# Decode attention with an FFN: W_down loaded by 1 KB rows, and one V tile loaded in five pieces instead of one

## The chip, the cores and the metric

The kernel runs on one core of one Trainium2 chip. The metric is the device time of one execution in microseconds (us), lower is better, taken as the median of several executions. On one core no other die is there to compare with, so a kernel's runs are called fast when they agree with each other; all timed runs here did (the widest spread is that of vsplit_only, 702.29 to 708.20 us). A kernel that was run only once has the state "unknown" and is compared with one run of the kernel before on the same chip.

## The reference, cut to what matters

```python
# x: (2, 1, 512)   k_cache, v_cache: (2, 32, 8192, 128)   all bf16
# wq: (512, 4096)  wo: (4096, 512)  W_gate, W_up: (512, 1376)  W_down: (1376, 512)
q = layernorm(x) @ wq                       # one query row per batch and head
p = softmax(q @ k_cache.T * 128 ** -0.5)    # over 8192 positions
h = x + (p @ v_cache) @ wo
n = layernorm(h)
g = n @ W_gate; u = n @ W_up
out = h + (relu(g) * u) @ W_down
```

K and V are 268 MB together. Each of their elements is used once, so the kernel is a stream of loads with most of the arithmetic hidden behind it (in the trace of the kernel before, DMA is 73% of the chain of work that ended last and VectorE 24%), and a short serial tail.

## The kernel before

The kernel goes through 32 pairs of heads. For each pair it loads one K tile and one V tile of 128 partitions by 32 KB (4 MB each) into four rotating slots. One row of a tile is one 32 KB packet in the trace. All loads but a small one of x are issued by SyncE into one queue (14,720 of the trace's 14,785 packets). A load of 128 partitions counts its semaphore up by 16 updates, which this document reads as one from each of the core's 16 DMA engines. Under this reading an engine takes its share of the loads one after the other: the first eight updates of V of pair 30 come 9.7 us after those of K of pair 31 (640.1 to 641.0 us after 630.4 to 631.3 us), which is eight rows of 1.213 us.

```python
def load(s, dst, src, eng=sp):
    slot_cnt[s] += 16
    eng.eng.dma_start(dst, src).then_inc(slot_sem[s], 16)
    return (slot_sem[s], slot_cnt[s])

def kv(cache, p):                      # 128 rows of 32 KB in the slot
    hp, b = divmod(p, B)
    return cache[b, 2 * hp:2 * hp + 2].rearrange("h (p j) d -> (h p) (j d)", p=64)

def load_v(p, parts=None):
    sv = (2 * p + 1) % 4
    if p >= 2:
        sp.wait(t_pv[p - 2])           # the slot is free
    if parts is None:
        t_v[p] = load(sv, slot[sv][:], kv(A_v_cache, p))      # one load, 128 partitions
        return
    src = kv(A_v_cache, p)             # the last pair only: four loads by columns
    for ci, (_, j0, j1) in enumerate(parts):
        nc.sync.dma_start(slot[sv][:, j0 * Dh:j1 * Dh],
                          src[:, j0 * Dh:j1 * Dh]).then_inc(sem_vl[ci], 16)
# ... cut: scores, softmax, PV
```

The end of the queue is what matters here. In the order of issue: K of pair 31, V of pair 30 (NP is 32), the two FFN weights W_up and W_gate, V of pair 31 in four column parts, W_down.

```python
# after the K tile of pair 30 is used up:
for k, w in enumerate((B_W_up, B_W_gate)):
    nc.sync.dma_start(slot[0][:, k * DC * F:(k + 1) * DC * F],
                      w.rearrange("(p c) n -> p (c n)", c=DC)).then_inc(sem_w, 16)
load_v(p + 1, vparts)                  # V of pair 31: columns 96-128, 0-48, 48-88, 88-96
nc.sync.dma_start(slot[0][:, 2 * DC * F:2 * DC * F + 10 * D],
                  B_W_down[0:10 * 128].rearrange("(p r) n -> p (r n)", r=10)).then_inc(sem_wd, 16)
# ... cut: PV of pair 30, output projection, PV of pair 31, layer norm
def ffn_in(dst, w, f0, f1):            # first layer: 88 matmuls for W_up and W_gate
    for f in range(f0, f1):
        fw = 128 if f < 10 else FR
        for c in range(DC):
            i = nc.tensor.matmul(dst[0:fw, f * B:(f + 1) * B],
                lhsT=w[:, c, f:1280:10] if f < 10 else w[:, c, 1280:F],   # every tenth column
                rhs=d_b[:, c * B:(c + 1) * B], start=(c == 0), stop=(c == DC - 1))
    return pe.run(i)
# ... cut: ReGLU
pe.wait((sem_wd, 32))                  # W_down, then 44 matmuls of the second layer
```

W_down lies in the slot with ten consecutive rows on a partition (10 KB in one piece), so hidden unit 10·p + r is on partition p. For that the first layer has to produce its units in the same order, and takes every tenth column of its weights.

The softmax here doesn't subtract the row's maximum and nothing guards it: scores larger than these inputs give would overflow.

Of the kernel before, what the change touches and what calls it, by code (L numbers as in the profile page):

```python
# [38 lines left out]
def bass_sequential_preLN__gqa_block_cached__glu_gated_reglu__decode_kernel(  # L39
# [10 lines left out]
    out: bass.AP,  # L50
):
    B, _, D = A_x.shape
    _, H, Sk, Dh = A_k_cache.shape
    F = B_W_gate.shape[1]
    assert (B, D, H, Sk, Dh, F) == (2, 512, 32, 8192, 128, 1376)
    DC = D // 128
    NP = B * H // 2
# [13 lines left out]
    with ExitStack() as es:  # L71
        def S(name):
            return es.enter_context(nc.semaphore(name))

        def sb(name, shape, dt):
            return es.enter_context(nc.sbuf_tensor(name, shape, dt))
# [11 lines left out]
        sem_x, sem_wq, sem_wo, sem_w, sem_wd, sem_out = S("x"), S("wq"), S("wo"), S("w"), S("wd"), S("out")  # L88
        sem_vl = [S(f"vl{i}") for i in range(4)]

        slot = [sb(f"slot{i}", [128, SLOT], BF16) for i in range(4)]
# [41 lines left out]
# [5 lines that stand above are left out]
        def kv(cache, p):  # L138
            hp, b = divmod(p, B)
            return cache[b, 2 * hp:2 * hp + 2].rearrange("h (p j) d -> (h p) (j d)", p=64)  # L140

        def tile(s):
            return slot[s][:].rearrange("p (j d) -> p j d", d=Dh)

        with nc.Block() as block:

            @block.sync
            def _(eng):
# [3 lines left out]
                t_k, t_v = {}, {}  # L152
# [99 lines left out]
                def score_group(p, g):  # L252
                    n = p * NG + g
                    pe.wait(t_ev[n])
                    if g == 0 and p >= 2:
                        pe.wait(t_exp[p - 2][0])
                    for k in range(GT):
                        jj = g * GT + k
                        i = nc.tensor.matmul(  # L259
                            Sp[p % 2][:, 2 * jj:2 * jj + 2], lhsT=kT[n % 3][:, k * 128:(k + 1) * 128],  # L260
                            rhs=qT[:, 2 * p:2 * p + 2], start=True, stop=True)
                    t_sc[n] = pe.run(i)
# [81 lines left out]
                def load_v(p, parts=None):  # L344
                    sv = (2 * p + 1) % 4
                    if p >= 2:
                        sp.wait(t_pv[p - 2])
                    if parts is None:
                        t_v[p] = load(sv, slot[sv][:], kv(A_v_cache, p))
                        return  # L350
                    src = kv(A_v_cache, p)
                    for ci, (_, j0, j1) in enumerate(parts):
                        nc.sync.dma_start(  # L353
                            slot[sv][:, j0 * Dh:j1 * Dh], src[:, j0 * Dh:j1 * Dh]).then_inc(sem_vl[ci], 16)

                for p in range(NP):
                    s = (2 * p) % 4
                    k_t = tile(s)

                    for c in range(NCH):  # L360
                        dve.wait(t_k[p])
                        if p == 0 and c == 0:
                            dve.wait(t_cp[NP // 4 - 1])
                        dve.last()
                        qv = q_b[:, p * Dh:(p + 1) * Dh].unsqueeze(1).broadcast_to([128, JC, Dh])
                        t_dm = dve.run(nc.vector.tensor_tensor(  # L366
                            out=prod[:], in0=k_t[:, c * JC:(c + 1) * JC, :], in1=qv, op=ALU.mult))
                        cur, w, tog = prod[:], Dh, 0
                        while w > 8:
                            half = w // 2  # L370
                            o = (tb[:, 0:JC * half].rearrange("p (j w) -> p j w", w=half) if tog == 0
                                 else prod[:, :, 0:half])
                            dve.last()
                            dve.run(nc.vector.tensor_tensor(  # L374
                                out=o, in0=cur[:, :, 0:half], in1=cur[:, :, half:w], op=ALU.add))
                            cur, w, tog = o, half, tog ^ 1
                        dve.last()
                        sc = scores[(p % 2) * NCH + c]
                        if p >= 2:
                            dve.wait(t_exp[p - 2][1 + c])  # L380
                        t_s = dve.run(nc.vector.tensor_reduce(out=sc[:], in_=cur, axis=AX.X, op=ALU.add))  # L381
                        if c == 0:

                            pe.wait(t_k[p])
                            for g in range(NG):
                                n = p * NG + g
                                if n >= 3:
                                    pe.wait(t_ev[n - 3])
                                for k in range(GT):
                                    j = NCH * JC + g * GT + k  # L390
                                    i = nc.tensor.transpose(  # L391
                                        Tp[n % 3][:, k * 128:(k + 1) * 128], k_t[:, j, :], ident[:])
                                t_pt[n] = pe.run(i)
                                act.wait(t_pt[n])
                                if n >= 3:
                                    act.wait(t_sc[n - 3])
                                t_ev[n] = act.run(nc.scalar.activation(  # L397
                                    out=kT[n % 3][:], in_=Tp[n % 3][:], func=ACT.Copy))
                                if g >= 1:
                                    score_group(p, g - 1)  # L400
                            score_group(p, NG - 1)
                            act.wait(t_sc[p * NG + NG - 1], t_const)
                            if p >= 2:
                                act.wait(t_pv[p - 2])
                            exp(p, 0, lambda q, a: Sp[p % 2][q, 0:2 * JP].rearrange("p (j a) -> p j a", a=2)[:, :, a],
                                NCH * JC, JP)
                        act.wait(t_s)
                        exp(p, 1 + c, lambda q, a: sc[q, :], c * JC, JC)
                    t_kfree[p] = (t_dm, t_pt[p * NG + NG - 1])


                    if p + 2 < NP:
                        sp.wait(*t_kfree[p])
                        t_k[p + 2] = load(s, slot[s][:], kv(A_k_cache, p + 2))
                    if p < NP - 2:
                        pv(p)
                        if p == W_AT:
                            pe.wait((sem_wo, 16), t_O[0], t_O[1], t_O[2])
                            t_om = pe.run(o_proj(range(0, HM), 0, 2))
                        if p < NP - 4:  # L420
                            load_v(p + 2)
                        elif p == NP - 3:
                            load_v(p + 1)
                    elif p == NP - 2:

                        sp.wait(*t_kfree[p])
                        for k, w in enumerate((B_W_up, B_W_gate)):
                            nc.sync.dma_start(  # L428
                                slot[0][:, k * DC * F:(k + 1) * DC * F],
                                w.rearrange("(p c) n -> p (c n)", c=DC)).then_inc(sem_w, 16)  # L430
                        load_v(p + 1, vparts)
                        nc.sync.dma_start(
                            slot[0][:, 2 * DC * F:2 * DC * F + 10 * D],
                            B_W_down[0:10 * 128].rearrange("(p r) n -> p (r n)", r=10)).then_inc(sem_wd, 16)


                pv(NP - 2)
# [31 lines left out]
                def ffn_in(dst, w, f0, f1):  # L469
                    for f in range(f0, f1):  # L470
                        fw = 128 if f < 10 else FR
                        for c in range(DC):
                            i = nc.tensor.matmul(  # L473
                                dst[0:fw, f * B:(f + 1) * B], lhsT=w[:, c, f:1280:10] if f < 10 else w[:, c, 1280:F],
                                rhs=d_b[:, c * B:(c + 1) * B], start=(c == 0), stop=(c == DC - 1))
                    return pe.run(i)

                FH = 6
                t_u = ffn_in(Sp[1], wup, 0, FC)
                t_g = (ffn_in(Op[1], wgt, 0, FH), ffn_in(Wp, wgt, FH, FC))  # L480

                dve.last()
# [78 lines left out]
```

## Time and profile before

| | before |
|---|---|
| time, median of 3 runs | 679.57 us (679.33 to 679.94) |
| span of the profiled run | 678.2 us |
| mean rate of the DMA engines | 416 GB/s; about 430 in most slices |
| K of pair 31 in | 630.4 to 631.3 us on eight engines, 635.2 to 636.8 us on the other eight |
| V of pair 30 in | 646.83 us |
| the V part of pair 31 that TensorE waits for | 664.23 us |
| W_down in | 667.94 us, needed at 672.8 us |

The times at which loads are in are read from the trace's semaphore updates: each load of 128 partitions counts a semaphore up by 16 steps, read here as one from each engine.

The first view is the page's summary of the DMA engines: the span in 40 slices of some 17 us, first the busy share in tenths, then the rate.

```profile
DMA  9999999999999999999999999999999999999991
GB/s 375 427 432 376 430 431 430 429 428 430 428 429 430 432 430 432 430 432 427 430 428 429 426 429 427 431 432 432 431 432 430 429 431 425 429 429 393 416 406 58
...
q8 instruction: 51, 0.84, 0.5%
```

The engines are busy throughout. The row of rates is near 430 GB/s but for a few slices. q8 is the queue that the page labels "instruction": 51 packets of 16 KB, 1.06 us each on average, 0.5% of the engines' time.

The second view is the chain of work that ended last, in order of time: start, duration, what.

```profile
640.14 24.09 DMA slot<-in_A_v_cache_dram
...
664.28 1.45 PE O L334 x48
...
667.34 2.79 PE S L473 x44
670.13 1.39 PE O L473 x24
671.51 1.25 PE W L473 x20
...
672.82 1.49 PE O L515 x44
```

After the last loads are issued, at 640 us, everything hangs on one load for 24 us. The rest is 10 us of serial work: 48 matmuls of PV (line 334), output projection and layer norm, the first FFN layer (line 473, 5.4 us), the second (line 515).

The third view is the timeline of TensorE in the tail: start, duration, engine, line, operation, count, and in brackets how long the engine was idle and for what.

```profile
664.28 1.44 PE L334 MATMUL O<-e,slot 128*128 128x2 bf16 x48 [1.63 <-DMA slot<-in_A_v_cache_dram]
...
667.34 2.79 PE L473 MATMUL S<-d_b,slot 128*128 128x2 bf16 x44 [0.34 <-DVE d_b L458]
...
672.68 1.48 PE L515 MATMUL O<-hd,slot 128*128 128x2 bf16 x40
```

TensorE waits 1.6 us for V of pair 31, and not at all for W_down before line 515.

The fifth view groups TensorE's weight loads by line and shape: busy time in us, then the mean of one in ns.

```profile
L334 PEld LDWEIGHTS O<-e,slot 128*128 128x128 bf16 x4096 | 114.5, 104 | 243.9 <-ACT e L267 122.8 <-issue 119.5 <-DMA slot<-in_A_v_cache_dram 1.7
...
L473 PEld LDWEIGHTS S<-d_b,slot 128*128 128x128 bf16 x40 | 2.4, 156 | 0.4 <-issue 0.4
...
L515 PEld LDWEIGHTS O<-hd,slot 128*128 128x128 bf16 x40 | 1.4, 118 | 0.0
```

A weight load from contiguous columns (line 334) takes 104 ns by this measure, one with every fourth column (line 515) 118, one with every tenth (line 473) 156. The starts of consecutive ones are 26.7, 33.4 and 58.3 ns apart.

### The profile page before, as it was taken

The page shows a single profiled execution, that of the slowest core. Times are in us where ns is not written, and L with a number is a line of the kernel's source. Part 1 is how long each engine was busy: PE and PEld are TensorE (multiplying, and loading weights), DVE is VectorE, ACT ScalarE, POOL GpSimd, SP SyncE. Part 2 cuts the span into 40 slices and gives each one's busy share as a digit, 9 for nine tenths or more (in the row PEclk, how much of TensorE's full clock was granted, in tenths as well). Part 3 has the DMA queues.
Part 4 walks back from the last instruction along what each step waited for, and adds up shares of the span by engine and source line. Part 5 has one row for each costly group of instructions (what it writes and reads, how often), then busy time and mean ns, then how long its engine had stood idle before and what let it go on. Part 6 is the DMA issues. An engine that isn't in the chain of part 4 may idle for free.

```text
span 678.2 us, 14430 instructions
## 1 busy us (share of the span) xinstructions
PE 297.5 (44%) x6596; PEld 269.5 (40%) x6596; DVE 493.6 (73%) x428; ACT 202.3 (30%) x523; POOL 1.7 (0%) x11
## 2 busy tenths in 40 slices
PE   2552254344544424454443435444344634433356
PEld 2442244333434424343443334434334634433355
DVE  1774577778777768877777787776788867777981
ACT  0630332233333213333322333332223333222430
POOL 0000000000000000000000000000000000000000
PEclk9999999556556556556555565555565555555555
DMA  9999999999999999999999999999999999999991
GB/s 375 427 432 376 430 431 430 429 428 430 428 429 430 432 430 432 430 432 427 430 428 429 426 429 427 431 432 432 431 432 430 429 431 425 429 429 393 416 406 58
DMA packets 14785, 281.97 MB, mean 416 GB/s; under 512 B 1443, under 2 KB 5637, under 8 KB 5765
## 3 DMA queue, kind: packets, MB, share of 16 engines
q1 hardware_dynamic: 14720, 281.06, 97.4%
q8 instruction: 51, 0.84, 0.5%
q14 instruction: 10, 0.07, 0.0%
q10 hardware_dynamic: 4, 0.00, 0.0%
HBM read 281.05 MB, written 0.00 MB: 414 GB/s over the span
## 4 chain that ended last, share of the span: by engine, by line
DMA 73%; DVE 24%; PE 1%; issue 1%; SPq 0%; DVEq 0%
DMA slot<-in_A_k_cache_dram 69%; DVE prod L366 15%; DVE tb L374 5%; DMA slot<-in_A_v_cache_dram 4%; DVE prod L374 3%; DVE scores L381 1%; PE S L473 0%; PE O L515 0%; PE O L334 0%; PE O L473 0%; PE W L473 0%; SPq L353 0%; SPq L135 0%; SPq L428 0%; PE W L309 0%
## 5 line engine op out<-in xcount | busy, mean ns | idle before, releaser
L366 DVE TENSOR_TENSOR prod<-slot,q_b 128x6144 bf16<-128x6144 bf16 x64 | 214.9, 3358 | 132.3 <-DMA slot<-in_A_k_cache_dram 131.1
L334 PE MATMUL O<-e,slot 128*128 128x2 bf16 x4096 | 118.7, 165 | 239.7 <-ACT e L267 120.2
L334 PEld LDWEIGHTS O<-e,slot 128*128 128x128 bf16 x4096 | 114.5, 104 | 243.9 <-ACT e L267 122.8
L397 ACT ACTIVATE kT<-T 128x1024 bf16<-128x1024 bf16 x128 | 126.8, 1022 | 169.9 <-PE T L391 168.8
L391 PE MATMUL T<-ident,slot 128*128 128x128 bf16 x1024 | 123.4, 307 | 76.7 <-DMA slot<-in_A_k_cache_dram 75.2
L374 DVE TENSOR_TENSOR tb<-prod 128x3072 bf16<-128x3072 bf16 (+1 forms) x128 | 148.2, 1158 | 4.4
L391 PEld LDWEIGHTS T<-ident,slot 128*128 128x128 bf16 x1024 | 100.2, 141 | 79.7 <-DMA slot<-in_A_k_cache_dram 78.2
L267 ACT ACTIVATE e<-scores 64x48 bf16<-64x48 f32 x128 | 32.8, 256 | 253.6 <-DVE scores L381 252.0
L374 DVE TENSOR_TENSOR prod<-tb 128x1536 bf16<-128x1536 bf16 (+1 forms) x128 | 84.2, 658 | 4.4
L259 PE MATMUL S<-qT,kT 128*128 128x2 bf16 x1024 | 48.4, 168 | 38.6 <-ACT kT L397 37.3
L259 PEld LDWEIGHTS S<-qT,kT 128*128 128x128 bf16 x1024 | 41.0, 107 | 57.4 <-ACT kT L397 57.4
L381 DVE TENSOR_REDUCE scores<-prod 128x48 f32<-128x384 bf16 x64 | 35.4, 553 | 2.2
L267 ACT ACTIVATION_READ_ACCUMULATOR e<-scores 64x1 f32 x128 | 23.6, 185 | 0.0
L267 ACT ACTIVATE e<-S 64x32 bf16<-64x32 f32 x64 | 13.0, 203 | 15.1 <-PE S L259 14.3
L267 ACT ACTIVATION_READ_ACCUMULATOR e<-S 64x1 f32 x64 | 12.8, 201 | 0.7
L241 ACT ACTIVATE q_b<-O 128x512 bf16<-128x512 f32 x8 | 4.3, 596 | 15.5 <-PE O L236 15.5
L212 DVE CAST qT<-W 128x64 bf16<-128x64 f32 x1 | 0.2, 225 | 11.9 <-PE W L207 11.9
L309 PE MATMUL W<-O_sb,X 128*128 128x2 bf16 (+1 forms) x136 | 5.0, 172 | 7.0 <-DVE O_sb L297 7.0
L309 PEld LDWEIGHTS W<-O_sb,X 128*128 128x128 bf16 x136 | 4.8, 118 | 7.2 <-DVE O_sb L297 7.2
L207 PE MATMUL W<-xlT,X 128*128 128x2 bf16 x128 | 3.6, 165 | 8.5 <-DMA X<-in_A_wq_dram 8.5
L207 PEld LDWEIGHTS W<-xlT,X 128*128 128x128 bf16 x128 | 3.5, 104 | 8.6 <-DMA X<-in_A_wq_dram 8.6
L285 DVE TENSOR_REDUCE zr<-O 128x16 f32<-128x48 f32 (+1 forms) x4 | 0.8, 204 | 8.3 <-PE O L277 8.3
(58 smaller groups left out, 44.4 us busy)
## 6 DMA issues: line engine op xcount, KB each, us to landing
slot<-in_A_k_cache_dram SPq DMA_DIRECT2D x32, 4096.0 KB, 27.8
slot<-in_A_v_cache_dram SPq DMA_DIRECT2D x31, 4096.0 KB, 32.1
X<-in_A_wq_dram SPq DMA_DIRECT2D x1, 4096.0 KB, 12.2
X<-in_A_wo_dram SPq DMA_DIRECT2D x1, 4096.0 KB, 49.0
slot<-in_A_v_cache_dram SPq DMA_DIRECT2D x1, 1536.0 KB, 21.6
slot<-in_B_W_up_dram SPq DMA_DIRECT2D x1, 1376.0 KB, 9.8
slot<-in_B_W_gate_dram SPq DMA_DIRECT2D x1, 1376.0 KB, 16.3
slot<-in_A_v_cache_dram SPq DMA_DIRECT2D x1, 1280.0 KB, 24.1
```

What stands on the lines that cost most here:

```text
L207: i = nc.tensor.matmul(Wp[:, h * B:(h + 1) * B], lhsT=wq[:, c, h * Dh:(h + 1) * Dh], rhs=lT[:, c * B:(c + 1) * B], start=(c == 0), stop=(c ...
L241: t_cp[m] = act.run(nc.scalar.activation(out=q_b[:, m * 512:(m + 1) * 512], in_=Op[m % 2][:], func=ACT.Copy))
L259: i = nc.tensor.matmul(Sp[p % 2][:, 2 * jj:2 * jj + 2], lhsT=kT[n % 3][:, k * 128:(k + 1) * 128], rhs=qT[:, 2 * p:2 * p + 2], start=True, ...
L267: t = act.run(nc.scalar.activation(out=e_t[p % 2][q, j0:j0 + nj, a], in_=src(q, a), func=ACT.Exp, scale=inv_sqrt_dh, accum_out=zs[q, 2 * p ...
L285: dve.run(nc.vector.tensor_reduce(out=zr[:, 2 * p0:2 * p1], in_=zbank(k)[:, 64:64 + n * (NCH + 1)].rearrange("p (n k) -> p n k", k=NCH + 1 ...
L309: i = nc.tensor.matmul(Wp[:, c * B + b0:c * B + b1], lhsT=wo_m[:, h, c, :], rhs=Ov[:, h // 2, h % 2, b0:b1], start=first[0], stop=last, sk ...
L334: i = nc.tensor.matmul(Op[k % 2][:, col:col + 2], lhsT=v_t[:, j, :], rhs=e_t[p % 2][:, j, :], start=(nmm == 0), stop=(nmm == J - 1))
L366: t_dm = dve.run(nc.vector.tensor_tensor(out=prod[:], in0=k_t[:, c * JC:(c + 1) * JC, :], in1=qv, op=ALU.mult))
L374: dve.run(nc.vector.tensor_tensor(out=o, in0=cur[:, :, 0:half], in1=cur[:, :, half:w], op=ALU.add))
L381: t_s = dve.run(nc.vector.tensor_reduce(out=sc[:], in_=cur, axis=AX.X, op=ALU.add))
L391: i = nc.tensor.transpose(Tp[n % 3][:, k * 128:(k + 1) * 128], k_t[:, j, :], ident[:])
L397: t_ev[n] = act.run(nc.scalar.activation(out=kT[n % 3][:], in_=Tp[n % 3][:], func=ACT.Copy))
```

## The change

There are two changes, with separate intents.

1. W_down is loaded by rows of 1 KB, so that hidden unit 128·r + p is on partition p. The first layer can then take 128 contiguous columns, and its weight loads should start 26.7 ns apart, as those of line 334 do, instead of 58.3.
2. V of pair 30 is loaded as four loads of 8 partitions and one of 96. A small load is taken to run on 8 of the 16, so the engines no longer all get the same bytes. The intent is to take rows off the eight engines that end late, and so to bring both groups to the end together.

```diff
                     if parts is None:
-                        t_v[p] = load(sv, slot[sv][:], kv(A_v_cache, p))
+                        n = 32 if p == NP - 2 else 0
+                        for a in range(0, n, 8):
+                            load(sv, slot[sv][a:a + 8], kv(A_v_cache, p)[a:a + 8])
+                        t_v[p] = load(sv, slot[sv][n:], kv(A_v_cache, p)[n:])
                         return
@@
-                            slot[0][:, 2 * DC * F:2 * DC * F + 10 * D],
-                            B_W_down[0:10 * 128].rearrange("(p r) n -> p (r n)", r=10)).then_inc(sem_wd, 16)
+                            slot[0][:, 2 * DC * F:2 * DC * F + 10 * D].rearrange("p (r n) -> p r n", n=D),
+                            B_W_down[0:10 * 128].rearrange("(r p) n -> p r n", p=128)).then_inc(sem_wd, 16)
@@
-                                dst[0:fw, f * B:(f + 1) * B], lhsT=w[:, c, f:1280:10] if f < 10 else w[:, c, 1280:F],
+                                dst[0:fw, f * B:(f + 1) * B], lhsT=w[:, c, f * 128:f * 128 + fw],
```

## The prediction

> **What bounds the kernel now.** The DMA engines. The page has them at 90% or more in all slices but the last, at about 430 GB/s; 281 MB at that rate is some 650 of the 678 us. The chain of waits is 73% DMA. Only its end matters here: the last V part that PE waits for lands at 664.23 us, PE having idled 1.7 us (timeline); then come 48 matmuls, the output projection, 88 matmuls of the FFN's first layer (667.34 to 672.77), 44 of the second, the store.
>
> The 16 semaphore steps of each load, read from the trace, show two groups. K of pair 31 is in on eight engines by 631.3, on the other eight only from 635.2 to 636.8; W_down by 661.1 and from 666.0 to 667.9. [...]
>
> **What changes.**
> 1. Weights of the FFN's first layer become contiguous. Their loads start 58.3 ns apart now (stride 10); contiguous ones of the same form (PV) start 26.7 ns apart. 80 x 31.6 ns = 2.5 us, all on the chain.
> 2. W_down in 1 KB rows: the W_o load, also 1 KB rows, took about 12 us for 256 KB per engine against 9.71, so 80 KB costs 0.7 us more. It is needed some 2 us after it lands: off the chain.
> 3. V of pair 30. [...]
> 4. Against that: [...]
>
> **Predicted.** [...]688 us, 8 in 10 between 675 and 699. Faster by over 2%: 1%; within 2%: 70%; slower by over 2%: 29%.
>
> **What would show it.** (1) The first layer's 88 matmuls take 2.9 us instead of 5.4. (2) PE doesn't wait for W_down. (3) The 32 KB packets of V of pair 30 stretch to several us on eight engines, DMA GB/s drops near 630 to 655 us, and PE's wait for V of pair 31 exceeds 10 us. [...]
>
> **What would make it wrong.** [...]PE or DVE, not V, last in the good case.

The sum was 679.6 us for the kernel before, less 2.5 us for the matmuls, plus 12.5 us for V of pair 31 landing later: about 690 us. The 12.5 us was the author's estimate, not worked out from anything measured. Three other cases: 697 us if the engines that get the extra rows are the late ones; and, if the small loads cost nothing by themselves, 675.4 us, or 680 us if the extra rows fall on the late engines. The 688 us weighs them.

## More of the kernel before

The fourth view gives busy times for stretches of time; PEclk is the granted TensorE clock, and the last two columns are the busy share of the DMA engines and their rate in GB/s.

```profile
core 0: us, PE busy (x) PEld busy (x) DVE busy (x) ACT busy (x) POOL busy (x), PEclk, DMA share, GB/s
630.00:650.00 20.00, 9.10 (x174) 8.06 (x172) 19.34 (x18) 9.14 (x23) 0.00 (x0) 0.50 0.99 413
650.00:676.00 26.00, 15.06 (x372) 14.52 (x369) 11.06 (x26) 1.33 (x8) 0.00 (x0) 0.50 0.52 213
```

## The result, and the profile after

| | before | after |
|---|---|---|
| time, median | 679.52 us (679.33 to 679.94, 4 runs) | 705.41 us (702.03 to 705.94, 4 runs) |
| span of the profiled run | 678.2 us | 703.4 us |
| K of pair 31 in, late engines | 636.83 us | 649.06 us |
| V of pair 30 in | 646.83 us | 675.55 us |
| V part of pair 31 in | 664.23 us | 691.98 us |
| first FFN layer, 88 matmuls | 5.4 us | 2.9 us |

The changed kernel is slower: the ratio is 1.037, with a 95% interval of 1.0337 to 1.0403. A ratio here is the mean time of one kernel's fast runs over that of the other's of the same rounds, so it is not quite the ratio of the medians. The prediction said 688 us, with a range to 699; the result is outside it. The place is as predicted, the size is not. The direction was only leaned to: 688 us lies above 679.6, but the prediction gave 70% to a change within 2% and 29% to the slower class that came.

The page's summary of the DMA engines, after:

```profile
DMA  9999999999999999999999999999999999999991
GB/s 388 417 414 393 424 435 427 433 430 427 431 428 432 426 436 427 428 433 425 437 422 440 421 437 423 433 430 430 430 428 431 427 429 431 425 366 147 198 329 65
```

The busy digits have not changed at all. The rates have: the three slices from about 633 to 686 us show 147, 198 and 329 GB/s. The busy share is made up of the times of the packets, and these have grown with the fall of the rate: a 32 KB packet that starts from 640 to 644 us takes 4.70 us after the change and 1.35 us before (table below).

The chain after:

```profile
639.77 48.45 DMA slot<-in_A_v_cache_dram
...
688.27 1.44 PE O L334 x48
689.71 2.27 another core or an unknown queue
...
692.03 1.45 PE O L334 x48
...
695.09 1.52 PE S L476 x44
...
698.06 1.48 PE O L518 x44
```

Issue happens at the same time (639.77 against 640.14 us), and the work behind the wait is shorter. Only the wait has grown. "Another core or an unknown queue" at 689.71 us is the next V part, whose semaphore update (691.98 us) the chain did not match to its load.

TensorE's timeline after:

```profile
675.60 3.58 PE L334 MATMUL O<-e,slot 128*128 128x2 bf16 x128 [20.53 <-DMA slot<-in_A_v_cache_dram]
...
684.48 1.01 PE L334 MATMUL O<-e,slot 128*128 128x2 bf16 x32 [2.38 <-DMA slot<-in_A_v_cache_dram]
...
688.27 1.44 PE L334 MATMUL O<-e,slot 128*128 128x2 bf16 x48 [2.78 <-DMA slot<-in_A_v_cache_dram]
...
692.03 1.44 PE L334 MATMUL O<-e,slot 128*128 128x2 bf16 x48 [2.31 <-DMA slot<-in_A_v_cache_dram]
...
695.09 1.52 PE L476 MATMUL S<-d_b,slot 128*128 128x2 bf16 x44 [0.35 <-DVE d_b L461]
...
697.92 1.47 PE L518 MATMUL O<-hd,slot 128*128 128x2 bf16 x40
```

TensorE waits 20.5 us for V of pair 30, and then 2.4, 2.8 and 2.3 us for parts of V of pair 31, 28.0 us in all, against 1.6 us before. Lines 476 and 518 are the former 473 and 515: the first layer takes 1.52 us where it took 2.79 us for the same 44 matmuls, and the second layer starts without a wait.

Stretches of time and weight loads after:

```profile
630.00:650.00 20.00, 3.42 (x48) 3.00 (x47) 13.29 (x13) 4.51 (x15) 0.00 (x0) 0.50 1.05 165
650.00:676.00 26.00, 4.46 (x73) 3.77 (x71) 14.17 (x12) 6.12 (x16) 0.00 (x0) 0.50 0.96 211
```

```profile
L518 PEld LDWEIGHTS O<-hd,slot 128*128 128x128 bf16 x40 | 1.4, 117 | 0.0
L476 PEld LDWEIGHTS S<-d_b,slot 128*128 128x128 bf16 x40 | 1.1, 104 | 0.4 <-issue 0.4
```

From 630 to 650 us the engines move 165 GB/s where they moved 413. The weight loads of the first layer take 104 ns, like the contiguous ones of line 334.

The packet records of the trace say how long one 32 KB row takes. The mean over all engines, for packets that start in the given stretch:

```
                    632-636 us   640-644 us
before                 1.21         1.35
after                  3.11         4.70
```

Of the 32 KB packets that start from 632 to 644 us, the shortest took 2.89 us after the change, against a mean of 1.24 us before it. So no engine went on at the old pace, and rows of K of pair 31 are among the slow ones, though it stands ahead of the small loads in the queue and is an ordinary load of 128 partitions. The last of its engines ends 12.2 us later than before. The prediction had no place for this: it expected long packets on eight engines only.

### The profile page after: what moved, and what is told of

It reads as the page before. It is cut to its first block, busy times and chain, and to the rows that moved or that the text cites. A ratio compares the mean times of both kernels' runs of the same rounds, so it can differ in the third digit from the quotient of the medians.

```text
span 703.4 us, 14434 instructions
## 1 busy us (share of the span) xinstructions
PE 295.0 (42%) x6596; PEld 266.7 (38%) x6596; DVE 493.7 (70%) x428; ACT 202.1 (29%) x523; POOL 1.7 (0%) x11
## 4 chain that ended last, share of the span: by engine, by line
DMA 74%; DVE 24%; PE 1%; issue 1%; SPq 0%; another core or an unknown queue 0%; DVEq 0%
DMA slot<-in_A_k_cache_dram 67%; DVE prod L369 14%; DMA slot<-in_A_v_cache_dram 7%; DVE tb L377 5%; DVE prod L377 3%; DVE scores L384 1%; PE O L334 0%; PE S L476 0%; PE O L518 0%; SPq L135 0%; SPq L431 0%; PE W L476 0%; PE O L476 0%; PE W L309 0%
```

## The experiments

The comparison with the reference passed for every run, those included that put V rows on wrong partitions or leave rows out. Presumably attention over 8192 nearly equal weights averages V so strongly that the comparison does not notice. So "correct" says nothing about the runs that are wrong, and they serve only for timing.

The theory at the outset: the cost comes from the destination, because the rows of a small load go to 8 adjacent partitions. An expected value without a label is that of the destination theory, and the author's estimate. Rivals: the cost comes from the source side (eight engines reading adjacent rows), from the uneven bytes per engine, or from the W_down rows. Later, when the size was not explained: the 96-partition load has a cost of its own.

### Each part alone: wdown_only and vsplit_only

wdown_only keeps the one V load of 128 partitions and has the rest of the change. vsplit_only has the five V loads and nothing else:

```diff
-                        t_v[p] = load(sv, slot[sv][:], kv(A_v_cache, p))
+                        n = 32 if p == NP - 2 else 0
+                        for a in range(0, n, 8):
+                            load(sv, slot[sv][a:a + 8], kv(A_v_cache, p)[a:a + 8])
+                        t_v[p] = load(sv, slot[sv][n:], kv(A_v_cache, p)[n:])
```

> W_down by 1 KB rows and contiguous first-layer weights alone, V of pair 30 in one load again. If the loss of 26 us is all in the split of V, this is faster than before by the matmuls' part: the after profile shows the first layer at 2.9 us instead of 5.4, so about 677.0 us. If the 1 KB rows of W_down hurt (they follow V of pair 31 in the queues), PE waits for W_down and it stays at or over 679.5 us.

> The split of V of pair 30 alone. If the two parts add up, 705.4 + 2.5 = about 708 us. If the two parts meet in the queues (1 KB rows behind the disturbed loads), clearly less than 708.

Measured: wdown_only 677.34 us (677.03 to 677.82, 5 runs; ratio 0.9966, interval 0.9953 to 0.9978), with 679.59 us for the kernel before in the same rounds. vsplit_only 705.18 us (702.29 to 708.20, 4 runs; ratio 1.0374, interval 1.0347 to 1.0402).

The timeline of TensorE in wdown_only:

```profile
664.66 1.44 PE L334 MATMUL O<-e,slot 128*128 128x2 bf16 x48 [1.59 <-DMA slot<-in_A_v_cache_dram]
...
667.72 1.52 PE L473 MATMUL S<-d_b,slot 128*128 128x2 bf16 x44 [0.35 <-DVE d_b L458]
...
670.55 1.48 PE L515 MATMUL O<-hd,slot 128*128 128x2 bf16 x40
```

The first layer runs as in the changed kernel, and nothing waits before line 515. W_down is in at 668.64 us against 667.94 us, 0.7 us later as predicted, and it is needed at 670.55 us, so 1.9 us were to spare. The packet records agree: an engine's 80 packets of 1 KB took 48.4 ns each, 3.9 us in all, where its 8 packets of 10 KB had taken 388 ns each, 3.1 us. This part of the change is worth 2.25 us. That is well under the 2% at which a run is called faster, but clear of the noise, and wdown_only is the fastest of the kernels with a right result.

The split alone costs 25.6 us (705.18 less 679.59). The two parts should then give 703; the changed kernel's 705.41 lies inside the spread of vsplit_only's own runs, so the 2.25 us can't be seen under it.

### Which partitions: step4, adj_to_step, step_to_adj

The same bytes in loads of the same size, but the eight rows of a small load lie four partitions apart. step4 steps both sides. The other two step only one side, so they leave V rows on wrong partitions.

```diff
-    load(sv, slot[sv][8 * a:8 * a + 8], V[8 * a:8 * a + 8])      # vsplit_only, for a in 0..3
+    load(sv, slot[sv][a:32:4],          V[a:32:4])               # step4
+    load(sv, slot[sv][a:32:4],          V[8 * a:8 * a + 8])      # adj_to_step
+    load(sv, slot[sv][8 * a:8 * a + 8], V[a:32:4])               # step_to_adj
```

> As the split of V alone, but each small load takes partitions a, a+4, .. a+28 of the first 32 (rows likewise)[...]. [...](adjacent destination partitions): the 32 KB packets of the small loads stay near 1.2 us, and the total falls from 708 to about 680 to 692, the rest being the 96-row load. Source theory (eight adjacent 32 KB rows read at once): the same fall, since the rows are spread too. Theory that loads of only 8 engines, or unequal bytes, are slow in themselves: still about 708.

> Wrong result on purpose: the small loads read eight adjacent rows (as in the change) but write partitions a, a+4, .. a+28 (as in the stepped run). [...]like the stepped run, about 697 us. Source theory (adjacent rows in HBM): like the split of V alone, about 705 us.

> Wrong result on purpose, the mirror: the small loads read rows a, a+4, .. a+28 and write eight adjacent partitions. [...]about 705 us, 32 KB packets near 3 us from 632 us on. Source theory: about 697 us, packets below 2 us there.

| destination \ source | adjacent rows | rows in steps of 4 |
|---|---|---|
| adjacent partitions | 705.18 us (vsplit_only) | 707.51 us (step_to_adj, one run) |
| partitions in steps of 4 | 698.13 us (adj_to_step, one run) | 696.68 us (step4, 4 runs, 696.22 to 698.32) |

The destination decides and the source does not. Stepping the destination takes back 8.5 us (705.18 less 696.68). It doesn't take back the other 17.1 us (696.68 less 679.59): step4's ratio is still 1.0247 (interval 1.0231 to 1.0262). The adjacent destination of the small loads is part of the cost, and something else is a larger part.

### Which engines are late: engine_map

Sixteen tiny loads of 1 to 16 partitions, each with a semaphore of its own, are queued behind K of pair 31. In the trace the load of n partitions, for n below 16, shows one update at its issue and n later ones. No record here carries an engine's number. The author assumed that each load uses the engines of the load before it and one more. If so, each further load adds one engine, and the time of the added update says whether that engine is early or late.

```diff
                         t_k[p + 2] = load(s, slot[s][:], kv(A_k_cache, p + 2))
+                        if p + 2 == NP - 1:
+                            for n in range(1, 17):
+                                nc.sync.dma_start(probe[0:n, (n - 1) * 32:n * 32],
+                                                  kv(A_v_cache, 0)[0:n, 0:32]).then_inc(sem_m[n - 1], 16)
```

> The kernel before with 16 tiny loads (64 bytes by 1, 2, .. 16 partitions, a semaphore each) queued behind K of pair 31. [...] If they are mixed, as the landings in the profile after suggest (about six early and two late), the premise that this split moves bytes from the late eight to the early eight is false. Time within 1 us of before.

Measured: 680.45 us (one run). From the semaphore updates of the trace:

```
partitions   updates from engines, us
 5           630.88 631.03 631.44 631.53 631.61
 6           631.07 631.20 631.62 631.71 631.79 636.84
 7           631.26 631.38 631.80 631.89 631.99 636.91 637.04
 8           630.70 631.45 631.56 631.99 632.07 632.16 637.12 637.24
 9           630.91 631.32 631.64 631.74 632.17 632.25 632.35 637.32 637.45
10           one more, late (636.97); 11 to 15 likewise (635.20 to 636.76)
16           one more, early (630.73)
```

The load of 8 partitions has six early updates and two late ones (637.12 and 637.24 us). If the engines are numbered from 0 in the order in which they are added, which is all that a number means here, 0 to 4, 7, 8 and 15 are early, and 5, 6 and 9 to 14 late. So the premise of the change does not hold: a load of 8 partitions does not keep clear of the late engines. By estimate, 128, 96 and 8 rows spread evenly over the engines of their 16, 16 and 8 updates, the extra rows would bring six late engines sooner, but the other two later by 2.4 us (two rows of 1.21 us), and V is in when its last engine is. By this count the split could not have gained even if the small loads had cost nothing else. The trace of vsplit_only fits it: of the 16 updates of the V part of pair 31 that TensorE waits for, 14 are in by 685.55 us, and two follow at 689.45 and 690.12 us. In halves (below), which has no load of 8 partitions, the last two come within 1.1 us of the 14th. So an estimated 2.4 us of what the split costs are the two extra rows on two late engines, and not the adjacent destination.

### Meant as equal bytes on all engines: r32_96 and halves

Both split V of pair 30 in two. They are meant to give all 16 engines the same bytes (2 + 6 rows, or 4 + 4). For the 96 rows the 16 updates in the trace of the changed kernel fit this; for 32 and 64 partitions it is the assumption.

```diff
+    load(sv, slot[sv][0:32], V[0:32]); t_v[p] = load(sv, slot[sv][32:], V[32:])      # r32_96
+    for a in (0, 64): t_v[p] = load(sv, slot[sv][a:a + 64], V[a:a + 64])             # halves
```

> V of pair 30 as one load of partitions 0 to 31 and one of 32 to 127[...]. [...]as in the stepped run (packets near 2.4 us), so V of pair 30 takes about 19 us instead of 9.7 and the total is about 689 to 693 us. If unequal bytes or loads on 8 engines cause the rest of the loss: back to about 680 us.

> V of pair 30 as two loads of partitions 0 to 63 and 64 to 127[...]. [...]32 KB packets take about 2.4 us and V of pair 30 takes 19.4 us instead of 9.7: about 689 us. If only loads on few engines or the number 96 are at fault: about 680 us.

Measured: r32_96 699.90 us, halves 696.08 us (one run each; before 679.98 us). These lose 20 and 16 us without any load of 8 partitions, so, if their bytes are even, uneven bytes are not the main cause. 32 KB packets take 2.51 us in halves from 632 to 636 us, twice the 1.21 us of before. At twice the time of a packet each half would take an estimated 9.7 us instead of 4.85 (four rows of 1.213 us), some 10 us in all; V of pair 31 is in 15.9 us later (680.13 us). So the loads around them lose as well.

### Loads by themselves in the middle of the kernel: probe_a and probe_b

In mid-stream all loads have 128 partitions, so one odd load stands alone there, and one run tests three of them. V of pairs 8, 14 and 20 is loaded only in part; the times of these two runs mean little, the packets are what counts.

```diff
# probe_a
+    p == 8:  for a in range(0, 32, 8): load(sv, slot[sv][a:a + 8], V[a:a + 8])     # four small loads, adjacent
+    p == 14: for a in range(4):        load(sv, slot[sv][a:32:4], V[a:32:4])       # four small loads, stepped
+    p == 20: load(sv, slot[sv][32:128], V[32:128])                                 # the 96 rows
# probe_b
+    p == 8:  load(sv, slot[sv][0:64], V[0:64])
+    p == 14: for a in (0, 32): load(sv, slot[sv][a:a + 4], V[a:a + 4])             # partitions 0 to 3 and 32 to 35
+    p == 20: for a in (0, 32): load(sv, slot[sv][a:a + 16:4], V[a:a + 16:4])       # the same number, in steps of 4
```

> Wrong result on purpose: at three pairs in the quiet middle of the kernel before, V is loaded only in part, so that one kind of load is seen by itself. Pair 8: the four loads of 8 adjacent partitions. Pair 14: the same as four stepped loads. Pair 20: partitions 32 to 127. [...]at pair 8 [...]the 32 KB packets of the other engines, which go on to K, stay at 1.2 us. [...]at pair 8 all packets lengthen to about 3 us for some 15 us. Both: pair 14 stays at 1.2 us. Pair 20 shows whether a 96-row load alone is slow[...].

> Wrong result on purpose, as the probe before. Pair 8: V of partitions 0 to 63 alone. Pair 14: partitions 0 to 3, then 32 to 35[...]. Pair 20: the same with step 4 (partitions 0, 4, 8, 12, then 32, 36, 40, 44[...]). [...]at pair 14 [...]packets of the other twelve stay at 1.2 us; at pair 20 all stay at 1.2 us. [...]at pair 14 the other engines' packets lengthen as well.

Both texts weigh two answers: the first given is that an odd load leaves the pace of the others alone, the second that it slows them too. Both are guesses beforehand.

Measured: probe_a 693.54 us, probe_b 669.57 us (before 679.85 us). The 32 KB packets of all engines, with the ordinary loads around the odd one:

```
                                          stretch, us   mean us of a packet
probe_a pair 8   four small, adjacent      190-204          2.24
probe_a pair 14  four small, stepped       306-330          1.24
probe_a pair 20  96 rows                   417-450          2.34
probe_b pair 8   64 rows                   191-205          2.57
probe_b pair 14  4 + 4 rows, adjacent      311-318          3.34 (up to 4.95)
probe_b pair 20  4 + 4 rows, stepped       416-440          1.23
```

The rates in the same stretches, probe_b first and then probe_a:

```profile
300.00:311.00 11.00, 3.85 (x104) 3.36 (x102) 10.69 (x10) 3.31 (x10) 0.00 (x0) 0.50 1.02 430
311.00:318.00 7.00, 1.44 (x48) 1.36 (x48) 0.76 (x2) 0.67 (x4) 0.00 (x0) 0.50 1.11 173
416.00:440.00 24.00, 11.12 (x272) 10.13 (x272) 19.33 (x16) 7.32 (x23) 0.00 (x0) 0.53 0.99 420
```

```profile
306.00:330.00 24.00, 11.12 (x272) 10.12 (x272) 19.59 (x16) 6.12 (x16) 0.00 (x0) 0.50 0.97 408
416.00:440.00 24.00, 4.07 (x132) 3.94 (x133) 9.32 (x10) 1.92 (x11) 0.00 (x0) 0.50 1.04 245
440.00:451.00 11.00, 4.59 (x63) 3.90 (x60) 10.76 (x8) 5.46 (x12) 0.00 (x0) 0.50 0.99 216
```

Pair 14 of probe_b tells most. Eight rows, 256 KB, go to partitions 0 to 3 and 32 to 35. A load of 4 partitions has four later updates in engine_map, so read as engines, the twelve others are free for the ordinary loads. If the odd load held up only its own engines, three quarters of the traffic would go on at 1.21 us. Instead the whole core drops from 430 to 173 GB/s for 7 us. Of the 33 packets of 32 KB that start from 311.4 to 318.1 us, at most eight belong to the odd load, and the shortest took 1.71 us. Eight rows to partitions in steps of 4 (pair 20) leave the packets at 1.23 us and the rate at 420 GB/s (426 in the kernel before). Pair 20 also reads its rows in steps of 4, but the two-by-two table above found no effect of that. So eight rows to two blocks of four adjacent partitions held up the ordinary loads too, at least 25 packets of them; what it is that adjacent partitions share is not shown.

The 96-row load (pair 20 of probe_a) holds up others as well. It takes 34 us until the packets are back to normal, at 245 and 216 GB/s, and the ordinary K loads before and behind it are slow too. The four small loads, when stepped, show no cost in their packets (1.24 us, against 1.22 in the same stretch of the kernel before).

### Each kind of load alone at its place: rows96_alone and smalls_alone

To size the two costs where they occur, V of pair 30 is loaded as the 96 rows alone, or as the four small adjacent loads alone (both wrong).

```diff
+    p == 30: t_v[p] = load(sv, slot[sv][32:128], V[32:128])                                   # rows96_alone
+    p == 30: for a in range(0, 32, 8): t_v[p] = load(sv, slot[sv][a:a + 8], V[a:a + 8])       # smalls_alone
```

> V of pair 30 is loaded as the one load of partitions 32 to 127 alone; the four small loads are left out, so a quarter of V of pair 30 is stale (wrong on purpose; the comparison may not notice, since earlier runs with rows missing passed). Theory A (the 96-row load is slow by itself and holds up the loads around it): the kernel with stepped small loads lost 17 us, nearly all of it to this load, so this one still loses about that, less the 2.4 us of the 1 MB that is not moved (9.7 us for 4 MB): about 694 us, with the 32 KB packets above 2 us on average between 632 and 644 us and K of pair 31 fully in at about 643 us. Theory B (the cost comes from the small loads, or from their meeting the 96-row load): packets stay at 1.2 us and the time is 677 to 680 us.

> V of pair 30 is loaded as the four loads of 8 adjacent partitions alone, the other 96 partitions are left out (wrong on purpose). Theory A (adjacency of the small loads costs about 8.5 us, the difference of the adjacent and the stepped version, and holds up all engines): 679.7 + 8.5 - 7.3 for the 3 MB not moved, about 681 us, with the 32 KB packets at 2.3 to 3.3 us for some 15 us, also those of K of pair 31. Theory B (a load of 8 partitions holds up only its own engines[...]): 672 to 676 us, with the packets of the engines that are already in the next loads at 1.2 us. Theory C (all of the 25 us comes from the small loads): about 698 us.

Measured: rows96_alone 693.08 us, smalls_alone 689.80 us (one run each; before 679.52 us on the same chip). Their rates:

```profile
630.00:650.00 20.00, 7.14 (x102) 6.10 (x99) 18.41 (x16) 8.49 (x21) 0.00 (x0) 0.59 1.04 219
```

```profile
630.00:650.00 20.00, 4.03 (x54) 3.58 (x51) 13.90 (x13) 4.94 (x16) 0.00 (x0) 0.50 0.95 170
```

rows96_alone came out as the theory had it (694 us; packets 2.47 us from 632 to 636 us). smalls_alone did not: I had put the small loads at 8.5 us, from the difference between adjacent and stepped ones, and so at 681 us. They cost more by themselves. To compare the versions, the rows that are not moved, or moved in addition, have to be allowed for, at 1.213 us a row. What counts is the engine that comes in last. In the versions with small loads this is taken to be one of the two late engines of the load of 8 partitions in engine_map (in smalls_alone, 14 of 16 updates of the V part are in by 666.73 us, the last two at 673.30 and 673.88). By the same even spread over the engines of the 16 or 8 updates, such an engine moves 8 rows of a whole tile, 6 in rows96_alone, only 4 in smalls_alone, and 10 in step4 and vsplit_only. The costs are estimates from that:

| V of pair 30 as | time, us | rows of the last engine against 8 | cost, us |
|---|---|---|---|
| four small adjacent loads alone | 689.80 | 4 fewer, 4.9 us | 689.80 + 4.9 − 679.52 = 15.2 |
| 96 rows alone | 693.08 | 2 fewer, 2.4 us | 693.08 + 2.4 − 679.52 = 16.0 |
| four small stepped loads and 96 rows (step4) | 696.68 | 2 more, 2.4 us | 696.68 − 2.4 − 679.59 = 14.7 |
| four small adjacent loads and 96 rows (vsplit_only) | 705.18 | 2 more, 2.4 us | 705.18 − 2.4 − 679.59 = 23.2 |

Stepped small loads add nothing to the 96 rows (14.7 against 16.0, with one run of rows96_alone), which agrees with probe_a, where their packets showed no cost. Adjacent ones cost 15.2 us alone but only some 7 to 8.5 us on top of the 96 rows: the sum of the two, 31.2 us, is 8 us more than both together, so they run into the same time.

smalls_alone also shows who is held up. K of pair 31, queued ahead, is in at 648.31 us instead of 636.83. No row of K or V kept its pace: the shortest 32 KB packet that starts from 632 to 644 us took 2.91 us. The 11 KB rows of W_up and W_gate, queued behind, slowed too: 26 such packets start from 630 to 646 us and take 1.30 us on average, against 0.44 us in the kernel before.

### All runs together

| run | what V of pair 30 is | time, us | V part of pair 31 in, us | packets 640–644, us |
|---|---|---|---|---|
| before | one load, 128 partitions | 679.52 | 664.23 | 1.35 |
| wdown_only | the same | 677.34 | 664.62 | 1.36 |
| after | 4 × 8 adjacent, 96 | 705.41 | 691.98 | 4.70 |
| vsplit_only | the same | 705.18 | 690.12 | 4.42 |
| step_to_adj | the same destination, wrong source rows | 707.51 | 691.68 | 4.61 |
| step4 | 4 × 8 stepped, 96 | 696.68 | 682.73 | 2.78 |
| adj_to_step | the same destination, wrong source rows | 698.13 | 682.51 | 2.86 |
| r32_96 | 32, 96 | 699.90 | 683.93 | 3.35 |
| halves | 64, 64 | 696.08 | 680.13 | 2.54 |
| rows96_alone | 96 rows only | 693.08 | 677.40 | 2.76 |
| smalls_alone | 4 × 8 adjacent only | 689.80 | 673.88 | 4.28 |

The times of wdown_only, after, vsplit_only and step4 are medians, the last two columns are of each kernel's profiled run. The time follows the moment at which V of pair 31 is in: the rest is 14 to 16 us with the strided weights and about 13 with the contiguous ones.

## Why the prediction was right or wrong

**The matmul part: right.** Predicted −2.5 us; the first layer went from 5.4 to 2.9 us, and wdown_only gained 2.25 us of time.

**W_down by 1 KB rows: right.** Predicted 0.7 us later and off the chain; measured 0.7 us later (0.8 us by its packets), 1.9 us to spare.

**Adjacent destination partitions cost time: right in kind.** The two-by-two table shows that stepping the destination helps (696.68 and 698.13 us against 705.18 and 707.51) and stepping the source doesn't, and probe_b that two blocks of four adjacent partitions lower the rate to 173 GB/s where eight stepped ones leave it at 420. The mechanism by which the prediction came to it is not shown.

**The engines that lose rows: the premise was false.** The prediction left open whether the eight engines of a small load are the early ones and gave 2.4 us for either answer. They are mixed: of the eight updates in engine_map six are early, two late, and a load is in when its last engine is. So it is the second answer that held, by estimate some 2.4 us lost. The rest of the split costs about ten times that, 23.2 us.

**The step that failed: the 12.5 us for V of pair 31, queued behind the split.** It is the term of the sum that is the author's estimate without a measurement. V of pair 31 was in 27.75 us later in the changed kernel (691.98 against 664.23), and the V split alone cost 25.6 us of time. Put in its place, 679.6 + 25.6 − 2.25 is 703 us, against 705.41 us measured. With two late engines among the eight of a small load, the prediction's own branch for that case, 697 us, is the fairer one to compare with: it has V some 20 us later (697 − 679.6 + 2.5), still 5.7 us short of the 25.6. The term was mis-sized in these places:

- The 96-row load was given only a small, unsized part of the 12.5 us. It costs some 16.0 us by itself, packets take twice as long while it runs (2.47 us from 632 to 636 us, against 1.21), and the loads around it slow down (K and V at 245 and 216 GB/s in probe_a). This is the largest omission.
- The four small loads alone cost an estimated 15.2 us (smalls_alone), 3.8 us each. The author's estimate for them was near that, but the prediction took off a part, expecting engines that drift apart to recover it. That was not shown: no recovery is seen.
- The model let only the engines wait that move the small loads. In the changed kernel no engine keeps its pace (shortest packet 2.89 us). That is why K of pair 31, ahead in the queue, came 12.2 us later, and why the other engines could not make up for it. For two loads of four adjacent partitions probe_b shows this hold-up directly (shortest packet 1.71 us); that it is also what makes the 96-row load slow is not shown.

Of the prediction's own test points, the first two came true, and of the third the drop in rate in the stretch that it named. The rest of the third did not come as worded: packets stretched everywhere and not on eight engines, and the long wait of TensorE, 20.5 us, was for V of pair 30. For V of pair 31 it waited 7.5 us, not over 10.

**What stays open.** Why the 96-row load is slow is not shown; the trace doesn't record which partition a packet writes. Why adjacent destination partitions cost time, and where the hold-up takes place, can't be told from packet durations. It is also open why the two costs overlap by 8 us and not more or less; both costs alone rest on one run each. A version that moves rows off the late engines without a hold-up was not tried: in engine_map loads of up to five partitions have early updates only, and late ones join with the 6th, 7th and 10th to 15th partition, so a larger load of this kind takes in late engines too.

## What to carry to other kernels

In a stream that runs at the limit of the DMA engines (about 430 GB/s here), keep every load on all 128 partitions: one 4 MB tile in pieces of 8, 64 or 96 partitions cost 16 to 26 us here. Two loads of four adjacent partitions each took the core's rate from 430 to 173 GB/s for 7 us, ordinary loads included. Read the rate in GB/s and the time of a packet, not the busy share, which stayed at 90% or more while the rate fell to 147 GB/s. Before bytes are moved between engines, find out by a row of tiny loads how many of a load's updates come late; and test the parts of a change one by one, as here one part gained 2.25 us while the other lost more than ten times that.
